# Block-sorted attention and a gated MLP on one core: a new order of issue for chunks 1 to 7, with packed score products

## The chip, the cores and the metric

The kernel runs on one core of a Trainium2 chip. A core has a matmul engine (TensorE, PE in the profile; its weight loads are listed apart as PEld), a vector engine (VectorE, DVE), an activation engine (ScalarE, ACT), a general-purpose engine (GpSimd, POOL) and an engine that here issues DMA transfers (SyncE, SP). Each of them runs its own list of instructions in the order in which the program gives them; semaphores hold an instruction until its inputs are there or its buffer is free. The metric is the time of one execution on the device in microseconds (us).

## The reference

The inputs are q, k and v of shape (4, 8, 768, 64), a net of 8x8 numbers for each of 32 heads, and two weight matrices. All is float32 outside the kernel; the kernel works in bfloat16 with float32 sums.

```python
P = sort_net                                   # 5 rounds of exp and row/column normalization
k_sorted = einsum('bhij,bhjcd->bhicd', P, k_b)  # blocks of 96 rows, mixed by P
v_sorted = einsum('bhij,bhjcd->bhicd', P, v_b)
scores = matmul(q_b, k_sorted^T) / sqrt(64)     # inside each block of 96 rows
attn = softmax(scores)
x = matmul(attn, v_sorted)                      # tokens x (8 heads * 64)
h = x @ w_in                                    # 512 -> 2048
out = (h * cos(h)) @ w_out                      # 2048 -> 512
```

## The kernel before

The 3072 tokens are worked on in eight chunks of 384 tokens; chunk n is one half of one batch, four blocks of 96 rows. Such a block of a chunk, with its eight heads, is called a unit (n, u). Batches 0 and 1 form group 0 (chunks 0 to 3), batches 2 and 3 form group 1 (chunks 4 to 7).

What is done for a unit, with the names of the kernel before and the lines that the profile gives:

- Scores, `qk`, `qk_half` or `s_ps`: eight matmuls (L405), one for each head. The turned queries lie in `q_turned` in such a way that for an even head rows 0 to 63 of the stationary operand hold the query and rows 64 to 127 are zero, and for an odd head the other way round; the moving operand (`keys_of`) has 128 rows of which the zeros leave 64 that count. Chunk 0 alone does its scores with operands of 64 rows (L681).
- The row maximum and the subtraction on DVE (L447 and L449, in chunks 0 and 1 L698 and L702), and the exponential on ACT (L467) into one of three `p_buf` tiles.
- The turn of the attention weights: by SP as a DMA transpose (L480), or on PE against the identity matrix (L713 or L493) with a copy out of PSUM by ACT.
- The product with the sorted values, `av_products` (L514), and on DVE the division by the row sums (L525, L527).
- The turn of x: by SP as a DMA transpose (L533), or on PE (L545, L722) with a copy.

For a chunk there follow eight steps `up` (L558; two column blocks of w_in each), a cosine on ACT (L562) and a product on DVE (L566) for each, and three output tiles `down` (L583) of sixteen matmuls each, with a copy out of PSUM and a store by SP (L573). The sorted keys and values are made by matmuls too (L375 and L425, L415), in pieces spread between the steps; `v_sort_g` makes those of group 1 with all 128 rows, two batches side by side.

PSUM has two pools: `big`, three tiles of two banks, and `acc`, two tiles of one bank.

The order is written out by hand, call after call for chunks 0 and 1, and with `moe_up`, `moe_down` and lists of calls for their slots for the others. PE works on the `up` and `down` steps of a chunk while the scores of the next one are made between them.

Two queues carry the transfers. POOL issues the loads: eight loads of 48 KB for the queries of a chunk from chunk 3 on (`load_q`, L129), and the keys and values of group 1 (`load_pair`, L92; two loads of 768 KB for keys, six of 256 KB for values). POOL also copies the loaded values into the order that the matmuls want (`v_permute`, L179), clears buffers, and has "holds": a copy of one column of a tile, which does nothing but keep POOL's later loads back until a transfer into that tile has landed (`hold`, L484; `hold_keys`, L393). SP issues the turns of q (`q_transpose_dma`, L149), of the attention weights and of x, and the stores.

The few lines that matter most for the order of POOL, in chunk 2:

```python
    p_hold(2, 2)
    for z in range(3, 6):
        load_pair(vbuf, vin_d, z * CD // 6, (z + 1) * CD // 6)
    load_q(4)
    v_permute(slice(0, 128))
```

Of the kernel before, what the change touches and what calls it, by code (L numbers as in the profile page):

```python
# [10 lines left out]
FP32 = mybir.dt.float32  # L11
# [3 lines left out]
AX = mybir.AxisListType  # L15


@with_exitstack
def kernel(
# [28 lines left out]
    IC = 4  # L48
# [323 lines left out]
    MH = H2 * IC  # L372

    def k_products(ps, t, c, rows, rhs, keys=kbuf):
        nc.tensor.matmul(  # L375
            ps[:, t], keys[rows, c * 2 * D:(c + 1) * 2 * D], rhs, start=True, stop=True)

    def k_sort_g(t0, eng, pool, tag):
        ps = pool.tile([128, 4, 4 * NB], FP32, name="ks", tag=tag)
        for t in range(4):  # L380
            k_products(ps, t, t0 + t, slice(0, 128), bds[1].rearrange("p x i -> p (x i)"),
                       pair)
        copy_on(
            eng, kT2[:, ::2, :, :, t0:t0 + 4].rearrange("p e b m t -> p b e m t"),
            ps.rearrange("p t (b e m) -> p b e m t", b=2, e=2))

    def k_swap(keys):
        nc.sync.dma_start(out=keys[:64, 1], in_=keys[64:, 0])
        nc.sync.dma_start(out=keys[64:, 1], in_=keys[:64, 2])

    def hold_keys():

        nc.gpsimd.tensor_copy(held[:], kT[1][:, 1, 0, :1])  # L393
# [14 lines left out]
    def v_cols(d, permuted):  # L408
        return vperm[:, d * blk:d * blk + 128] if permuted else vv[:, d]

    def v_sort_b(b, d0, nd, eng, pool, tag):
        ps = pool.tile([128, nd, 2 * NB], FP32, name="vs", tag=tag)
        rows, xs = slice(0, 64 + b * 64), slice(b * H, (b + 1) * H)
        for t in range(nd):
            nc.tensor.matmul(  # L415
                ps[:, t], v_cols(d0 + t, b == 1 or d0 + t >= D // 2)[rows],
                bdv[rows, xs].rearrange("p x i -> p (x i)"), start=True, stop=True)
        copy_on(
            eng, vS[0][:, b * 2 * NB:(b + 1) * 2 * NB, d0:d0 + nd],
            ps[:blk].rearrange("p t n -> p n t"))  # L420

    def v_sort_g(d0, nd, eng, pool, tag):
        ps = pool.tile([128, nd, 4 * NB], FP32, name="vs", tag=tag)
        for t in range(nd):
            nc.tensor.matmul(  # L425
                ps[:, t], v_cols(d0 + t, True), bds[1].rearrange("p x i -> p (x i)"),
                start=True, stop=True)
        copy_on(eng, vS[1][:, :, d0:d0 + nd], ps[:blk].rearrange("p t n -> p n t"))

    def v_at(g, b2, hp, h2, i):  # L430
        return (b2 * 2 + hp) * NB + h2 * nb + i


    LATE = 5
    s_t, pb, pT, xn_t = {}, {}, {}, {}
    xT = {}
    cnt = [0]

    def qk_part(n, u, part, pool, tag):
        w = len(part)  # L440
        sc = pool.tile([128, w, 512], FP32, name="sc", tag=tag)
        for h2 in range(H2):
            for e, hp in enumerate(part):
                scores(sc[:, e, h2 * 128:h2 * 128 + blk], n, u, h2, hp)
        scv = sc[:blk].rearrange("p e (h c) -> p (e h) c", c=128)[:, :, :blk]
        mx = small.tile([blk, w * H2], FP32, name="mx", tag="mx")
        nc.vector.reduce_max(mx[:], scv, axis=AX.X)  # L447
        s = s_t[n, u][:, part[0]:part[0] + w].rearrange("p e h c -> p (e h) c")
        nc.vector.tensor_tensor(s, scv, mx.to_broadcast(list(s.shape)), op=ALU.subtract)  # L449

    def qk(n, u):

        s_t[n, u] = sp.tile([blk, 2, H2, blk], FP32, name="s", tag="s")
        qk_part(n, u, [0, 1], big, "big")

    def qk_half(n, u, hp, pool=None, tag="acc"):

        if hp == 0:
            s_t[n, u] = sp.tile([blk, 2, H2, blk], FP32, name="s", tag="s")
        qk_part(n, u, [hp], pool or acc, tag)  # L460

    def expo(n, u, on_pe=False):
        p = p_bufs[cnt[0] % NP]
        cnt[0] += 1


        nc.scalar.activation(  # L467
            p[:, :, :blk], s_t.pop((n, u)).rearrange("p e h c -> p (e h) c"), AF.Exp,
            scale=scale)
        if n < LATE:  # L470
            t = ptp.tile([128, 2 * H2, blk], BF16, name="pT", tag="pT")
        else:

            z, w = (n * IC + u) % 8, 2 * H2 * blk
            t = vperm[:, z * w:(z + 1) * w].rearrange("p (a c) -> p a c", c=blk)
        pT[n, u] = t
        if on_pe:
            pb[n, u] = p
        else:
            nc.sync.dma_start_transpose(out=t[:], in_=p.rearrange("p a c -> p (a c)"))  # L480

    def hold(t):

        nc.gpsimd.tensor_copy(held[:blk], t[:blk, 0, :1])  # L484

    def p_hold(n, u):
        hold(pT[n, u])

    def p_transpose(n, u, eng, pool, tag):
        p = pb.pop((n, u))  # L490
        ps = pool.tile([128, 2 * H2, 128], BF16, name="pps", tag=tag)
        for a in range(2 * H2):
            nc.tensor.transpose(ps[:blk, a, :blk], p[:, a, :blk], ident[:blk, :blk])  # L493
        copy_on(eng, pT[n, u][:blk], ps[:blk, :, :blk])

    av_ps = {}

    def av(n, u, on_pe=False):
# [641 lines left out]
```

## Time and profile before

| | |
|---|---|
| median of 3 runs | 239.73 us (238.47, 239.73, 239.83) |
| span of the profiled execution, first to last instruction | 236.9 us |
| PE busy | 228.3 us, 96% |
| PEld, DVE, ACT, POOL busy | 61%, 72%, 65%, 39% |
| granted clock of the matmul engine, mean | 0.998 |
| bytes read from and written to HBM | 27.27 MB, 6.29 MB |

The execution that the profile shows is told by its span alone; a time of its own from start to end is not recorded beside it. The span is 2.8 us shorter than the median of the timed runs, and 1.6 us shorter than the fastest of them.

How to read the rows: an instruction group has its line, engine, operation, "written tile<-read tiles", shapes and count; after the bar stand its busy time in us, the mean duration of one in ns, and the idle time of the engine just before it with what ended that idle time. Matmuls are pipelined: each has a duration of some 200 to 380 ns from its start to its modelled end, but the next one starts long before that. So the time that a run of matmuls costs is read from start to start.

### The profile page before, as it was taken

Reading aid. Unit: us, or ns where it says so; the run is one execution under the profiler, and the core shown is the slowest. Engines: PE = TensorE matmul, PEld = TensorE weight load, DVE = VectorE, ACT = ScalarE, POOL = GpSimd, SP = SyncE. Lnnn points to the kernel's source line nnn. Section 1 sums busy time; section 2 is a strip of 40 time slices with the busy share of each in tenths; the row PEclk is TensorE's granted clock in tenths of the full one; section 3 lists DMA queues with packets and bytes.
Section 4 is the critical chain, followed back from the end, with each engine's and each line's share of the span. In section 5 each row is a group of like instructions: output and inputs, shape, how many; then the busy total and the mean of one; then the engine's idle time right before and its main releaser. Section 6 shows DMA issues by size and latency. Waiting matters only on the chain.

```text
span 236.9 us, 5429 instructions
## 1 busy us (share of the span) xinstructions
PE 228.3 (96%) x2230; PEld 144.0 (61%) x2230; DVE 171.1 (72%) x284; ACT 154.0 (65%) x205; POOL 93.4 (39%) x117
## 2 busy tenths in 40 slices
PE   8699999999999999999999999999999999999994
PEld 2368799567665656655666556655564565555553
DVE  5658976887789666893689976998698769535700
ACT  3356975588889747795688747673767376646611
POOL 7699994894970098940808000800000000000000
PEclk9999999999999999999999999999999999999999
DMA  7999999995899989869899938944972460341012
GB/s 97 203 199 205 203 224 211 148 201 167 102 117 183 146 155 136 160 150 184 95 104 101 116 64 150 209 68 91 119 216 46 80 192 3 55 133 47 0 44 89
DMA packets 66423, 30.89 MB, mean 130 GB/s; under 512 B 55136, under 2 KB 61920, under 8 KB 66144
## 3 DMA queue, kind: packets, MB, share of 16 engines
q0 software_dynamic: 24048, 13.64, 42.1%
q1 hardware_dynamic: 42064, 16.73, 33.4%
q8 instruction: 17, 0.28, 0.5%
q10 hardware_dynamic: 288, 0.20, 0.3%
q14 instruction: 6, 0.05, 0.1%
HBM read 27.27 MB, written 6.29 MB: 142 GB/s over the span
## 4 chain that ended last, share of the span: by engine, by line
PE 81%; DMA 6%; ACT 4%; DVE 4%; issue 3%; POOL 1%; SPq 0%; ACTq 0%; POOLq 0%
PE h L558 31%; PE o L583 21%; DMA pT<-p_buf 5%; PE h L735 5%; PE o L756 4%; PE sc L405 3%; PE av L514 3%; PE ks L375 2%; PE vs L662 2%; ACT p_buf L467 2%; PE o L1104 1%; PE vs L425 1%; PE pps L713 1%; DMA xT<-xn 1%; PE vs L238 1%
## 5 line engine op out<-in xcount | busy, mean ns | idle before, releaser
L558 PE MATMUL h<-xT,w_in_t 128*128 128x384 bf16 x448 | 78.4, 326 | 0.2 <-DMA xT<-xn 0.2
L583 PE MATMUL o<-w_out_t,gg 128*128 128x512 bf16 x320 | 76.5, 379 | 0.0
L566 DVE TENSOR_TENSOR gg<-c,h 128x768 bf16<-128x768 f32 x56 | 52.6, 949 | 18.8 <-ACT c L562 18.8
L562 ACT ACTIVATE c<-h,half_pi 128x768 f32<-128x768 f32 x56 | 50.4, 900 | 22.5 <-PE h L558 21.6
L558 PEld LDWEIGHTS <-w_in_t 128*128 128x128 bf16 x448 | 42.2, 98 | 26.5 <-issue 0.6
L583 PEld LDWEIGHTS <-gg 128*128 128x128 bf16 x320 | 29.1, 98 | 27.6
L467 ACT ACTIVATE p_buf<-s 96x768 bf16<-96x768 f32 x32 | 26.0, 840 | 4.4 <-DVE s L702 2.4
L179 POOL COPY vperm<-kv 64x1536 bf16<-64x1536 bf16 (+1 forms) x10 | 28.0, 2831 | 0.6 <-DMA kv<-in_v_dram 0.6
L449 DVE TENSOR_TENSOR s<-sc,mx 96x384 f32<-96x384 f32 (+1 forms) x33 | 24.3, 735 | 1.8
L447 DVE TENSOR_REDUCE mx<-sc 96x4 f32<-96x384 f32 (+1 forms) x33 | 24.0, 729 | 0.7 <-PE sc L405 0.7
L527 DVE TENSOR_TENSOR xn<-av,r 96x512 bf16<-96x512 f32 x32 | 22.0, 687 | 1.1
L525 DVE RECIPROCAL r<-av 96x8 f32<-96x8 f32 x32 | 6.4, 199 | 14.6 <-PE av L514 14.4
L129 POOL DMA_DIRECT2D kv<-in_q_dram x24 | 15.9, 674 | 0.7 <-issue 0.5
L405 PE MATMUL sc<-kTs,q_turned 128*128 128x96 bf16 x224 | 15.3, 206 | 0.1
L249 ACT COPY kv<-o 128x512 f32<-128x512 f32 (+2 forms) x10 | 5.3, 530 | 14.9 <-PE o L583 12.4
L405 PEld LDWEIGHTS <-q_turned 128*128 128x128 bf16 x224 | 12.6, 98 | 4.0 <-DVE s L449 0.4
L249 ACT CAST kTs<-ks 128x512 bf16<-128x512 f32 (+1 forms) x18 | 11.0, 632 | 5.7 <-PE ks L375 5.7
L756 PE MATMUL o<-w_out_t,gg 128*128 128x512 bf16 x48 | 11.4, 379 | 0.0
L251 DVE COPY kv<-o 128x512 f32<-128x512 f32 (+1 forms) x5 | 3.0, 602 | 11.4 <-PE o L1104 8.5
L129 POOL DMA_DIRECT2D q_mem<-in_q_dram x16 | 10.7, 684 | 1.2 <-DMA kv<-in_v_dram 1.0
L238 PE MATMUL idle<-warm 128*128 128x512 bf16 x29 | 8.5, 436 | 2.8 <-ACT q_turned L321 1.8
L735 PE MATMUL h<-xT,w_in_t 128*128 128x192 bf16 x128 | 11.1, 246 | 0.0
(119 smaller groups left out, 285.0 us busy)
## 6 DMA issues: line engine op xcount, KB each, us to landing
out_dram<-kv SPq DMA_DIRECT2D x12, 256.0 KB, 2.5
out_dram<-o_s SPq DMA_DIRECT2D x10, 256.0 KB, 2.7
w_in_t<-in_moe_w_in_dram POOLq DMA_DIRECT2D x4, 512.0 KB, 11.8
w_out_t<-in_moe_w_out_dram POOLq DMA_DIRECT2D x4, 512.0 KB, 12.6
kv<-in_k_dram POOLq DMA_DIRECT2D x2, 768.0 KB, 10.3
kv<-in_v_dram POOLq DMA_DIRECT2D x2, 768.0 KB, 13.1
pair<-in_k_dram POOLq DMA_DIRECT2D x2, 768.0 KB, 11.0
kv<-in_v_dram POOLq DMA_DIRECT2D x6, 256.0 KB, 5.4
```

Source lines behind the costliest of these rows:

```text
L129: nc.gpsimd.dma_start(out=q_heads[:, i, :, e], in_=src[:, ih * IC + i, :, e])
L179: nc.gpsimd.tensor_copy(dst, src)
L405: nc.tensor.matmul(out, q_of(n, hp)[:, x:x + 128], keys_of(n, u, h2, hp), start=True, stop=True)
L447: nc.vector.reduce_max(mx[:], scv, axis=AX.X)
L449: nc.vector.tensor_tensor(s, scv, mx.to_broadcast(list(s.shape)), op=ALU.subtract)
L467: nc.scalar.activation(p[:, :, :blk], s_t.pop((n, u)).rearrange("p e h c -> p (e h) c"), AF.Exp, scale=scale)
L527: nc.vector.tensor_tensor(xn.rearrange("p h e d -> p e h d"), avv[:, :, :, :D], r.to_broadcast([blk, 2, H2, D]), op=ALU.mult)
L558: nc.tensor.matmul(h[:, f2, :w], w_in_t[:, kk, f * 128:(f + 1) * 128], xT[n][:, kk], start=(kk == 0), stop=(kk == KC - 1))
L562: nc.scalar.activation(c[:], h[:, :, :w], AF.Sin, bias=half_pi[:, 0:1])
L566: nc.vector.tensor_tensor(gt[n, fp // 2][:, f:f + 2], c[:], h[:, :, :w], op=ALU.mult)
L583: nc.tensor.matmul(o[:], gt[n, f // 4][:, f % 4, ts * 128:(ts + 1) * 128], w_out_t[:, f, :], start=(f == 0), stop=(f == FC - 1))
L735: nc.tensor.matmul(o[:, part, f2 * w:(f2 + 1) * w], w_in_t[:, kk, f * 128:(f + 1) * 128], xT[0][:, kk, h * w:(h + 1) * w], start=(kk == 0) ...
```

## The change

The hand-written calls are replaced by one list of text lines, `PLAN`, and a loop that calls one function for each line. A line is an operation, its chunk and unit, and where it goes: `B` and `c` are the PSUM pools `big` and `acc`, `A` and `V` are ACT and DVE. `S` is a unit's scores, `M` the maximum, `X` the subtraction, `E` the exponential, `TP` and `TE` the turn on PE and its copy, `TD` the turn by DMA, `AV` the product with the values, `N` the division, `XP`, `XE` and `XD` the turn of x, `U`, `C`, `G` an `up` step with cosine and product, `D` four matmuls of a `down` tile, `O` and `W` its copy and its store; `QP`, `QE`, `QD` are the turns of q, `ks`, `kg`, `vb`, `vg` with `kse`, `kge`, `vbe`, `vge` the sorted keys and values and their copies, `Lq`, `Lpk`, `Lpv` the loads, `vp2` the copy of values into order, `hk`, `hp`, `hq` the holds; `nop` does nothing.

Chunk 0, and chunk 1 as far as its first `down` matmuls, are issued in the same order as before. From there on:

- Ten units have their scores from a new function `T`, which multiplies only the 64 rows that count: for the two heads of a pair one product uses rows 0 to 63 and the next rows 64 to 127, into two different PSUM banks. They stand on PE's list in five neighbouring pairs: (2,3) (2,2); (3,2) (3,3); (4,3) (5,0); (6,1) (6,0); (7,1) (7,2). The other units of chunks 1 to 7 keep products of 128 rows.
- One group of eight value columns of group 1 (`vg 0 8`) becomes `vgT`: two products of 64 rows in place of each one of 128 rows, one for each batch. It stands between the products of units (3,2) and (3,3).
- The turn of unit (1,0) is made by DMA (`TD 1 0`) in place of PE and a copy by ACT. On SP it stands behind the store `W 0 0`, which comes before `W 0 1` now.
- On every engine many operations change places by a few positions. No other operation is added or removed. Five copies change their engine: `kge 3`, `kge 6`, `vbe 0` go from ACT to DVE, `XE 2 1` and `O 3 2` from DVE to ACT; `kg 2`, `ks 0`, `vb 0` and `XP 3 1` change their PSUM pool.
- On SP the order of stores and turns changes too: W 0 0, TD 1 0, W 0 1 in chunk 1; QD 5 before W 2 2; W 3 2 before QD 6; W 4 0 before the turns of chunk 6; TD 6 1 before TD 6 0; XD 6 1 before XD 6 0.
- POOL's order from chunk 1 on was: zeros 3, Lq 3, hk, Lpv 0, Lpv 1, Lpv 2, zeros 4, hp 2 2, Lpv 3, Lpv 4, Lpv 5, Lq 4, vp2, ones 1, hp 3 3, Lq 5, hq 1, Lq 6, hq 0, Lq 7. It becomes: zeros 3, Lpv 2, Lq 3, zeros 4, Lpv 0, hk, Lpv 1, Lpv 3, Lpv 4, Lq 4, Lpv 5, vp2, hp 2 2, Lq 5, hp 3 3, ones 1, Lq 6, hq 1, Lq 7, hq 0.

```diff
--- before.py
+++ after.py
...
+PLAN = """\
...
+D 0 1 0
+D 0 1 1
+D 0 1 2
+X 1 2
+D 0 1 3
+M 1 0
+X 1 0
+M 1 3
+E 1 2 1
+E 1 0 2
+TP 1 2 B
+TE 1 2 A
+O 0 1 o A
+X 1 3
+E 1 3 0
+ks 4 B
+D 0 0 2
+D 0 0 3
+kse 4 V
+O 0 0 o V
+AV 1 2
+W 0 0
+S 1 1 B
+TP 1 3 c
+TD 1 0
+nop
+D 0 2 0
+D 0 2 1
+M 1 1
+X 1 1
+W 0 1
+TE 1 3 A
+D 0 2 2
+AV 1 3
+N 1 2
+N 1 3
+XP 1 2 B
+E 1 1 1
+TP 1 1 c
+XE 1 2 A
+AV 1 0
+D 0 2 3
+TE 1 1 A
+AV 1 1
+N 1 0
+XP 1 0 B
+N 1 1
+O 0 2 t A
+ks 3 B
+XE 1 0 A
+kse 3 A
+ks 2 c
+kse 2 A
+XP 1 3 c
+XE 1 3 V
+ks 1 B
+XP 1 1 B
+XE 1 1 V
+ks 0 c
+kse 1 A
+kse 0 A
+ks 5 B
+kse 5 V
+QP 2 0 c
+W 0 2
+QP 2 1 B
+QE 2 1 1 V
+zeros 3
+Lpv 2 6
+Lq 3
+zeros 4
+QE 2 1 0 V
+QE 2 0 1 V
+QE 2 0 0 V
+Lpv 0 6
+kswap 0
+hk
+U 1 0
+C 1 0
+G 1 0
+vb 0 B
+vbe 0 V
+vb 1 c
+vbe 1 A
+QD 3
+Lpv 1 6
+U 1 1
...
+S 2 1 c 1
+E 2 0 2
+nop
+TD 2 0
+M 2 1 1
+G 1 7
+X 2 1 1
+E 2 1 0
+TD 2 1
+D 1 0 0
+D 1 0 1
+T 2 3 B
+T 2 2 B
+M 2 2
+X 2 2
+nop
+D 1 0 2
+kg 0 c
+Lpv 3 6
+kge 0 A
+D 1 0 3
+O 1 0 o A
+M 2 3
+X 2 3
+Lpv 4 6
+E 2 2 1
+TD 2 2
+W 1 0
+kg 1 B
+D 1 1 0
+kg 4 B
+Lq 4
+Lpv 5 6
+kge 4 A
+kge 1 A
+vp2 0 128
+E 2 3 2
+hp 2 2
+D 1 1 1
+kg 2 c
+kge 2 A
+AV 2 0
+D 1 1 2
+D 1 1 3
+kg 3 B
+O 1 1 o A
+N 2 0
+W 1 1
+kge 3 V
+AV 2 1
+AV 2 2
+N 2 1
+TP 2 3 c
+N 2 2
...
+U 2 5
+C 2 5
+G 2 5
+kg 11 c
+kge 11 A
+kswap 1
+U 2 7
+C 2 7
+G 2 7
+nop
+U 2 6
+C 2 6
+E 3 0 0
+G 2 6
+S 3 1 c 1
+M 3 1 1
+X 3 1 1
+nop
+D 2 0 0
+E 3 1 1
+D 2 0 1
+D 2 0 2
+T 3 2 B
+vgT 0 8 B
+nop
+M 3 2
+T 3 3 B
+TD 3 0
+X 3 2
+TD 3 1
+D 2 0 3
+O 2 0 o A
+W 2 0
+M 3 3
+X 3 3
+E 3 2 2
+vge 0 8 A
+TD 3 2
+E 3 3 0
+D 2 1 0
+Lq 5
+D 2 1 1
+D 2 1 2
+vg 2 8 B
...
+TD 3 3
+D 2 1 3
+O 2 1 o A
+hp 3 3
...
+XE 3 3 V
+Lq 6
+nop
+D 2 2 3
+O 2 2 o V
+QD 5
+U 3 0
+C 3 0
+G 3 0
+hq 1
...
+D 3 0 0
+nop
+D 3 0 1
+X 4 2
+D 3 0 2
+nop
+E 4 0 1
+TD 4 0
+E 4 1 2
+nop
+TD 4 1
+T 4 3 B
+T 5 0 B
+E 4 2 0
+TD 4 2
+D 3 1 0
+M 4 3
+D 3 0 3
+X 4 3
+vg 15 4 B
+vge 15 4 A
...
+D 3 2 3
+O 3 2 v A
+W 3 2
+U 4 0
+QD 6
+Lq 7
...
+D 4 0 2
+nop
+T 6 1 B
+T 6 0 B
+M 6 0
+X 6 0
+D 4 0 3
...
+AV 6 2
+N 6 2
+XD 6 2
+nop
+T 7 1 B
+T 7 2 B
+D 5 1 2
...
+D 5 2 2
+XE 6 3 A
+U 6 0
+D 5 2 3
+O 5 2 v V
+E 7 1 2
+nop
+TD 7 1
+C 6 0
+G 6 0
+W 5 1
+U 6 2
...
+W 7 1"""
...
+    def T(n, u, pool, tag):
+        o = kept_tile(("s", n, u, None), pool, tag, [128, 2, 512], FP32, "sc")
+        for h2 in range(H2):
+            for hp in range(2):
+                rows, x = slice(hp * D, (hp + 1) * D), (u * H2 + h2) * blk
+                nc.tensor.matmul(
+                    o[:, hp, h2 * 128:h2 * 128 + blk], q_of(n, hp)[rows, x:x + 128],
+                    keys_of(n, u, h2, hp)[rows], start=True, stop=True)
...
+    def vgT(z, nd, pool, tag):
+        o = kept_tile(("vg", z), pool, tag, [128, 2, nd, 2 * NB], FP32, "vs")
+        for t in range(nd):
+            for b in range(2):
+                rows = slice(b * 64, (b + 1) * 64)
+                nc.tensor.matmul(
+                    o[:, b, t], v_cols(z * 4 + t, True)[rows],
+                    bds[1][rows, b * H:(b + 1) * H].rearrange("p x i -> p (x i)"),
+                    start=True, stop=True)
...
+    def E(n, u, z):
+        p = made["p", n, u] = p_bufs[z]
...
+    def TD(n, u):
+        nc.sync.dma_start_transpose(
+            out=p_to(n, u)[:], in_=made.pop(("p", n, u)).rearrange("p a c -> p (a c)"))
...
+    def Lpv(z, of):
+        load_pair(vbuf, vin_d, z * CD // of, (z + 1) * CD // of)
...
+    for line in PLAN.split("\n"):
+        name, *args = line.split()
+        given = []
+        for a in args:
+            given += words.get(a) or ((int(a),) if a.isdigit() else (a,))
+        calls[name](*given)
...
-    q_transpose(2, 1, (V, V), *B)
-    zeros_between(3)
-    load_q(3)
-    hold_keys()
-    load_pair(vbuf, vin_d, 0 * CD // 6, 1 * CD // 6)
-    load_pair(vbuf, vin_d, 1 * CD // 6, 2 * CD // 6)
-    load_pair(vbuf, vin_d, 2 * CD // 6, 3 * CD // 6)
...
-    expo(2, 3, True)
-    p_hold(2, 2)
-    for z in range(3, 6):
-        load_pair(vbuf, vin_d, z * CD // 6, (z + 1) * CD // 6)
-    load_q(4)
-    v_permute(slice(0, 128))
```

1372 lines of the change are left out of this document (817 added, 555 removed).

## Prediction

> **What bounds the kernel now.** I read the page first, then the chain of waits, then the timeline of PE around each place where it stops, and last the transfers. The first rows are the busy shares and the chain by engine, from the page.
>
> ```profile
> PE 228.3 (96%) x2230; PEld 144.0 (61%) x2230; DVE 171.1 (72%) x284; ACT 154.0 (65%) x205; POOL 93.4 (39%) x117
> ...
> PE 81%; DMA 6%; ACT 4%; DVE 4%; issue 3%; POOL 1%; SPq 0%; ACTq 0%; POOLq 0%
> ```
>
> PE is busy 96% of 236.9 us and carries 81% of the chain. A gain must take PE work away or close one of the few gaps; DVE and ACT have 28% and 35% of their time free. The next rows are PE's timeline at the four largest gaps of chunks 2 to 5 that the new order touches, and one more that it does not close.
>
> ```profile
> 72.82 1.89 PE L583 MATMUL o<-w_out_t,gg 128*128 128x512 bf16 x8
> 74.55 0.50 PE L405 MATMUL sc<-kTs,q_turned 128*128 128x96 bf16 x8
> 74.89 1.03 PE L583 MATMUL o<-w_out_t,gg 128*128 128x512 bf16 x4
> 75.94 0.38 PE L375 MATMUL ks<-bd,pair 128*128 128x128 bf16 x4
> ...
> 86.27 0.34 PE L545 MATMUL xps<-order,xn 96*128 96x96 bf16 x4
> 86.87 0.34 PE L545 MATMUL xps<-order,xn 96*128 96x96 bf16 x4 [0.27 <-DVE xn L527]
> ...
> 108.91 0.68 PE L514 MATMUL av<-vS,pT 96*128 96x65 bf16 x16
> 109.94 0.61 PE L425 MATMUL vs<-bd,vperm 128*128 128x128 bf16 x8 [0.34 <-ACT pair L249]
> 110.38 1.89 PE L583 MATMUL o<-w_out_t,gg 128*128 128x512 bf16 x8
> ...
> 140.03 0.43 PE L514 MATMUL av<-pair,pT 96*128 96x65 bf16 x8 [0.41 <-DMA pT<-p_buf]
> ...
> 165.78 0.59 PE L583 MATMUL o<-w_out_t,gg 128*128 128x512 bf16 x2
> 166.55 0.65 PE L558 MATMUL h<-xT,w_in_t 128*128 128x384 bf16 x3 [0.17 <-DMA xT<-xn]
> ```
>
> I count from start to start. Eight `down` matmuls take from 72.82 to 74.55, 0.216 us each; eight score products from 74.55 to 74.89, 42 ns each. Four `down` matmuls from 74.89 would be through at 75.75, but the next product starts at 75.94: 0.19 us are lost. In the same way four products of 42 ns from 86.27 lose 0.43, and two `down` matmuls from 165.78 lose 0.34. At 108.91 sixteen products with values stand; eight of that kind take 0.26 us (55.09 to 55.35, rows below), so 0.51 are lost before 109.94.
>
> **The packed products.** Here is PE's timeline in chunk 0, where products of 64 rows stand between products of 128 rows.
>
> ```profile
> 20.91 0.39 PE L238 MATMUL vs<-warm 128*128 128x512 bf16 x1
> 21.23 0.93 PE L662 MATMUL vs<-bdv,vperm 64*128 64x128 bf16 x14
> ...
> 22.06 0.40 PE L681 MATMUL sc<-kTs,q_turned 64*128 64x64 bf16 x14
> 22.39 0.28 PE L238 MATMUL pps<-warm 128*128 128x256 bf16 x1
> ```
>
> A unit's eight products of 128 rows take 0.34 us (above). The 64-row products step at (0.40 - 0.19)/13 = 16 ns: two of them run in the time of one. I take 42 ns for a pair of 96 columns, 0.17 us for a unit. A change between the two kinds has a price: from the 512-column product at 20.91 to the 64-row one it is 0.32 us, against the 0.216 of a stream, so 0.10; back, the last 64-row product starts at 22.27 and the next at 22.39, 0.09 more than a 64-column step. A neighbouring pair of units then costs 2 x 0.17 + 0.19 = 0.53 in place of 0.68: -0.15, five times -0.75 us. Bounds: -1.7 if the change were free, +0.95 if the halves did not overlap.
>
> `vgT`: eight products of 128 rows take from 109.94 to 110.38, 0.44 us; sixteen of 64 columns in pairs at 32 ns are 0.26: -0.18. It stands inside an island and pays no change of kind.
>
> **Gaps that close.** At 75.94 `kg 0` waited for the subtraction of (2,1); the list puts its maximum ahead of a product on DVE, so all 0.19 go. At 86.87 the division of (2,3) queued behind other DVE steps; that of (2,2) now comes early and one copy moves to ACT: 0.43 go. At 109.94 `vg 4` waited for a copy on ACT; the copies before it now start earlier: I keep 0.17, 0.34 go. At 166.55 a turn of x was late; half a unit's scores (0.17 us) now stands before that step: 0.2 go. Together -1.16 us, bounds 0 and -1.47. The gap at 140.03 stays.
>
> **The early turn by DMA.** Here is PE where the turned weights of (1,0) are used, with the turn of (1,1) before it and the next step behind, and SP.
>
> ```profile
> 54.73 0.52 PE L713 MATMUL pps<-ident,p_buf 96*96 96x96 bf16 x8
> 55.09 0.42 PE L514 MATMUL av<-vS,pT 96*128 96x65 bf16 x8
> 55.35 1.03 PE L756 MATMUL o<-w_out_t,gg 128*128 128x512 bf16 x4
> ```
>
> ```profile
> 49.20 2.44 SPq L573 DMA_DIRECT2D out_dram<-o_s  x2
> ```
>
> A turn on PE takes 0.36 us (54.73 to 55.09); that goes. Without the turn PE is at that product at 55.09 - 0.36 = 54.73. The DMA is queued behind `W 0 0`, which is the second of these two stores, issued at 51.31 (its copy on DVE ends then); so it goes out at about 51.7. What it meets there, from the answers for these stores, for the two key loads that POOL issued at 43.1 and 43.6, and for the later turns by DMA:
>
> ```profile
> L573 SPq DMA_DIRECT2D out_dram<-o_s x2: 332/350/368, 49.2 to 51.3; - x2
> ...
> DMA to landing us min/median/max: 5.9/6.6/7.4
> ```
>
> ```profile
> L92 POOL DMA_DIRECT2D pair<-in_k_dram x2: 553/558/562, 43.1 to 43.6; - x2
> ...
> DMA to landing us min/median/max: 9.2/11.0/12.7
> ```
>
> ```profile
> L480 SPq DMA_TRANSPOSE pT<-p_buf x11: 1212/1229/2490, 75.9 to 135.6; - x11
> ...
> DMA to landing us min/median/max: 2.8/3.0/4.5
> ```
>
> The key loads are in flight until 43.6 + 12.7 = 56.3, and the store issued at 51.31 landed at 57.2 (5.9 us). The turn takes the second store's place in the queue. If it met nothing it would land at 51.7 + 2.8 = 54.5, in time; by the store, its nearest row in place and time, at 56.8 or later. I take 56.8: PE waits 2.1 us, bounds 0 and 2.8. On PE all of chunk 1's rest is queued behind it. After that wait ACT has its copies (`O 0 2`, `XE 1 0`, `kse 3`, `kse 2`) in one go, and `ks 0` needs the bank that `kse 2` frees: I add 0.3 us, bounds 0 and 0.8.
>
> **POOL's loads without their hold.** These are POOL's timeline in chunk 2, SP's beside it, the answers for the turns of q of chunk 3, and the queues in 68 to 73 us.
>
> ```profile
> 60.74 5.33 POOL L129 DMA_DIRECT2D kv<-in_q_dram  x8
> ...
> 66.24 1.64 POOL L92 DMA_DIRECT2D kv<-in_v_dram  x3
> 67.85 1.88 POOL L137 MEMSET q_mem<- 96x1024 bf16 x2
> 82.91 0.18 POOL L484 CAST held<-pT 96x1 f32<-96x1 bf16 x1 [13.18 <-DMA pT<-p_buf]
> ```
>
> ```profile
> 75.93 5.14 SPq L480 DMA_TRANSPOSE pT<-p_buf  x3
> ```
>
> ```profile
> L149 SPq DMA_TRANSPOSE q_turned<-kv x2: 1577/2900/4222, 68.5 to 70.3; - x2
> ...
> DMA to landing us min/median/max: 6.2/6.4/6.7
> ```
>
> ```profile
> q0 software_dynamic: 424, 0.74, 98.0%
> q1 hardware_dynamic: 218, 0.06, 6.6%
> ```
>
> The hold (`hp 2 2`) kept POOL idle for 13.18 us, until the turns of chunk 2 had landed, and `Lpv 3` to `Lpv 5` and `Lq 4` came after. In the list that hold stands behind all of them and behind `vp2`; nothing else stops them. By the old durations `Lpv 2` starts at 60.74 (0.55 us), `Lq 3` ends at 66.6, `zeros 4` at 68.5, `Lpv 0`, the short `hk` and `Lpv 1` at 69.8, and `Lpv 3` goes out there. From 68 to 73 us three loads of values moved 0.74 MB, 0.15 MB/us, and the turns of q, issued at 68.5 and 70.3, got 0.06 MB: SP's transfers waited until POOL's were done. Four loads of values (1.0 MB) and `Lq 4` (0.38 MB), in flight from some 70 us, are through at about 79. The turn of (2,0), issued at 75.93, lands at 78.7 alone (2.8 us); its product stood at 79.53 and moves to some 79.2. The nearest row with such loads ahead is a store issued at 88.89:
>
> ```profile
> L573 SPq DMA_DIRECT2D out_dram<-o_s x1: 332/332/332, 88.9 to 88.9; - x1
> ...
> DMA to landing us min/median/max: 4.4/4.4/4.4
> ```
>
> ```profile
> out_dram<-c SPq DMA_DIRECT2D x1, 256.0 KB, 2.4
> ```
>
> That is 2.0 over a store of the same size with nothing ahead. With 2.0 more the turn lands at 80.7 and PE waits 1.5 us. Bounds: 0, and 4.5 if all that is queued goes first (to 79; then the turns of q, which needed from 73 to 70.3 + 6.2 = 76.5, so 3.5; then 1.2 of its own: 83.7).
>
> The Trainium skill has a rule against both waits: by "DMA: Bandwidth & Descriptors", Queues, rings and completion order, a DMA engine goes round robin between its queues, packet by packet. By it a turn would wait for one packet of a load and not for the load, and both waits would be near 0. The trace does not bear that out at 68 to 73 us, where the one queue had 98% and the other 6.6%.
>
> **The small rest.** `E 4 3` stands behind two copies of ACT, so the late turn at 140.03 gets later, and `U 6 0` is issued four `down` matmuls earlier, ahead of the landing of x: +0.4 together, bounds -0.4 and +1.5. `O 3 2` on ACT, the copies on DVE, the order of stores, and the earlier `Lq 5` to `Lq 7`: 0, covered by the 28% and 35% of free time and by loads that are wanted a chunk later.
>
> **The sum.** -0.75 - 0.18 - 1.16 - 0.36 + 2.1 + 0.3 + 1.5 + 0.4 = +1.85 us. The span is 236.9 and the median of the runs 239.73; I put the change on both: span 238.7, time 241.6 us.
>
> **The rivals.**
> - *Both turns land in time.* Then the two waits and the 0.3 behind the first fall away: 241.6 - 3.9 = 237.7 us, and 236.9 with the small rest at its lower end. For it: what the list removes on PE is certain. Against it: 5.9 to 7.4 us for stores at that very place.
> - *Only the first is late:* the turns of q get ahead of the loads, and the turn of (2,0) with them: 241.6 - 1.5 = 240.1.
> - *The whole backlog goes ahead of the turns of chunk 2.* The wait is 4.5 in place of 1.5: 244.6, slower. It decides as soon as `Lpv 3`, `Lpv 4` and `Lq 4` are queued before 75.9 and are served in the order of their issue. For it speak the 98% above, against it the 4.4 us of the store at 88.89.
> - *The halves do not overlap:* +0.95 in place of -0.75, 243.3. Against it speak the 16 ns of chunk 0.
>
> **Chances.** About 1% (2.4 us) is what this kernel's measurement can tell from no change. Forecast 0.34 (its own range 240.3 to 242.9, somewhat under half of it over 242.1, so 0.14); both in time 0.32 (half of it, 0.16, below 237.3, if a change of kind is cheaper too); first alone 0.18; backlog 0.12; no overlap 0.04. That makes 0.16 faster, 0.14 + 0.12 + 0.04 = 0.30 slower, and the other 0.54 within 1%. The range 236.8 to 244.0 leaves out the outer parts of the first and the third rival.
>
> **What would show it.** Ten units' products with a step near 21 ns and five islands at 0.53 us; the product of (1,0) waiting on `DMA pT<-p_buf` for about 2 us near 54.7; `Lpv 3` issued near 70 us and not behind a wait of 13 us; the turns of q of chunk 3 and of (2,0) landing late, and a wait of PE on `DMA pT<-p_buf` near 80 us. If the products of (1,0) and (2,0) start without a wait, the forecast is wrong and the first rival holds.

## The result and the profile after

The changed kernel took 253.31 us (median of 4 runs, 251.04 to 254.5) against 239.12 us of the kernel before: a ratio of 1.0581, 95% interval 1.0514 to 1.0649. It is 14.2 us slower, where +1.85 us (241.6 us) was forecast and the range ended at 244.0. A ratio and its interval, here and below, leave out executions more than 1.5% above the fastest of the same kernel; a median counts them all. The profiled execution took 251.04 us with a span of 249.2, so 12.3 us of span are to be explained.

The page after, with the same rows as of before, and the row of the granted clock in 40 slices:

```profile
PE 230.5 (92%) x2207; PEld 144.5 (58%) x2230; DVE 172.0 (69%) x285; ACT 153.2 (61%) x203; POOL 93.0 (37%) x117
...
PEclk9999999997999858999999999999999999999999
...
PE 66%; DMA 11%; issue 1%; POOL 1%; DVE 0%; ACT 0%; SPq 0%; ACTq 0%
```

PE's busy time rose by only 2.2 us, though PE has less to do; the chain now goes through DMA for 11% in place of 6%, and the clock is low in four slices. The waits of PE for transfers, and PE's timeline at the three long ones:

```profile
PE av L1445 <- DMA pT<-p_buf: 10.1, 3, 6.4
...
PE av L1445 <- DMA vperm<-p_buf: 0.7, 1, 0.7
```

```profile
54.38 0.52 PE L1427 MATMUL pps<-ident,p_buf 96*96 96x96 bf16 x8
56.90 0.43 PE L1445 MATMUL av<-vS,pT 96*128 96x65 bf16 x8 [2.00 <-DMA pT<-p_buf]
...
89.14 0.65 PE L1445 MATMUL av<-vS,pT 96*128 96x65 bf16 x8 [6.35 <-DMA pT<-p_buf]
89.60 3.60 PE L1550 MATMUL o<-w_out_t,gg 128*128 128x512 bf16 x8
...
147.48 0.42 PE L1445 MATMUL av<-pair,pT 96*128 96x65 bf16 x8
149.63 0.43 PE L1445 MATMUL av<-pair,pT 96*128 96x65 bf16 x8 [1.74 <-DMA pT<-p_buf]
```

The three are the products of (1,0), (2,0) and (4,2). Behind the second one, eight `down` matmuls are busy for 3.60 us; before, eight took 1.89. The stretches behind the first two waits, with the length and PE's busy time first and the granted clock (PEclk) behind the engines:

```profile
57.00:60.00 3.00, 2.94 (x36) 2.11 (x37) 1.60 (x4) 1.01 (x2) 0.00 (x0) 0.58 0.00 0
89.20:93.20 4.00, 4.00 (x18) 1.79 (x19) 0.89 (x2) 1.28 (x2) 1.05 (x1) 0.50 1.00 179
93.20:96.00 2.80, 2.75 (x32) 2.32 (x32) 2.20 (x5) 1.35 (x2) 2.80 (x2) 0.67 0.25 94
```

The clock lost 3.00 x 0.42 + 4.00 x 0.50 + 2.80 x 0.33 = 4.2 us. With 10.1 us of waits that is 14.3 us, against 12.3 in the span (behind the first row the clock stays low up to 60.9 us, which adds some 0.4). So what the new list saves on PE seems to be there, some 2 us net; this is what is left over of a sum, not a measurement of its own.

Why the turn of (2,0) came late is seen in SP's timeline, and in the queues from 81 to 84 us (packets, MB, share of 16 engines' time):

```profile
71.21 7.90 SPq L994 DMA_TRANSPOSE q_turned<-kv  x2
...
79.20 6.62 SPq L1418 DMA_TRANSPOSE pT<-p_buf  x3
```

```profile
q1 hardware_dynamic: 1219, 0.31, 81.6%
q0 software_dynamic: 1244, 0.16, 80.1%
```

POOL had issued its four loads of values and q for chunk 4 from 71.07 us on. SP needed until 79.1 to issue the two turns of q of chunk 3, one of them 5.9 us long, so the turn of (2,0) went out at 79.20 and landed at 89.09. From 81 to 84 us SP's queue (q1) and POOL's (q0) moved almost the same count of packets. It isn't so everywhere: from 77 to 80 us, with loads of values on their way, POOL's queue moved 265 packets (0.48 MB) and SP's 131 (0.03 MB), and from 51.8 to 53.0 us, behind the issue of the turn of (1,0), POOL's moved 37 packets of its key load (0.23 MB) and SP's none.

### The profile page after: what moved, and what is told of

The parts are those of the page before. It is cut to its first block, busy times and chain, and to the rows that moved or that the text cites. A ratio compares the mean times of both kernels' runs of the same rounds, so it can differ in the third digit from the quotient of the medians.

```text
span 249.2 us, 5406 instructions
## 1 busy us (share of the span) xinstructions
PE 230.5 (92%) x2207; PEld 144.5 (58%) x2230; DVE 172.0 (69%) x285; ACT 153.2 (61%) x203; POOL 93.0 (37%) x117
## 4 chain that ended last, share of the span: by engine, by line
PE 66%; DMA 11%; issue 1%; POOL 1%; DVE 0%; ACT 0%; SPq 0%; ACTq 0%
PE h L1505 28%; PE o L1550 25%; DMA pT<-p_buf 8%; PE av L1445 3%; PE sc L1344 2%; DMA vperm<-p_buf 2%; PE ks L1225 2%; PE o L1641 1%; PE xps L1479 1%; PE vs L1316 1%; DMA kTs<-kTs 1%; PE sc L1371 1%; POOL vperm L1024 1%; PE vs L1293 0%; DVE kTs L1096 0%
## 5 line engine op out<-in xcount | busy, mean ns | idle before, releaser
L1550 PE MATMUL o<-w_out_t,gg 128*128 128x512 bf16 x348 | 86.8, 387 | 1.1 <-issue 0.2
L1550 PEld LDWEIGHTS <-gg 128*128 128x128 bf16 x368 | 33.7, 100 | 33.8 <-issue 1.9
L1385 DVE TENSOR_REDUCE mx<-sc 96x8 f32<-96x768 f32 (+1 forms) x41 | 31.6, 771 | 1.9 <-PE sc L1344 1.1
L1445 PEld LDWEIGHTS <-pT 96*128 96x128 bf16 (+1 forms) x160 | 8.0, 109 | 13.0 <-DMA pT<-p_buf 11.3
L1445 PE MATMUL av<-vS,pT 96*128 96x65 bf16 (+1 forms) x128 | 7.3, 209 | 8.4 <-DMA pT<-p_buf 8.3
L1094 ACT COPY kv<-o 128x512 f32<-128x512 f32 (+2 forms) x11 | 5.9, 537 | 14.8 <-PE o L1550 12.2
L1094 ACT CAST kTs<-ks 128x512 bf16<-128x512 f32 (+1 forms) x16 | 9.8, 635 | 3.3 <-PE ks L1225 3.2
L1083 PE MATMUL idle<-warm 128*128 128x512 bf16 x28 | 9.7, 492 | 2.2 <-ACT q_turned L1166 1.2
L1094 ACT COPY xT<-xps 128x384 bf16<-128x384 bf16 (+1 forms) x11 | 5.5, 508 | 9.9 <-PE xps L1479 9.8
L1094 ACT CAST pair<-vs 96x512 bf16<-96x512 f32 (+1 forms) x12 | 8.7, 726 | 3.9 <-PE vs L1316 3.9
## 6 DMA issues: line engine op xcount, KB each, us to landing
kv<-in_k_dram POOLq DMA_DIRECT2D x2, 768.0 KB, 10.1
```

Source lines behind the costliest of these rows:

```text
L1094: eng.copy(dst, src)
L1385: nc.vector.reduce_max(mx[:], s_view(n, u, hp), axis=AX.XY if n < 2 else AX.X)
L1445: nc.tensor.matmul(a[:w, hp, h2 * (D + 1):(h2 + 1) * (D + 1)], pt[:blk, e * blk:e * blk + w], vS[g][:, v_at(g, b2, hp, h2, ih * IC + u), : ...
L1550: nc.tensor.matmul(out_ps[n, ts][:], gt[n, q][:, f % 4, ts * 128:(ts + 1) * 128], w_out_t[:, f, :], start=(f == 0), stop=(f == FC - 1))
```

## The experiments

All times are compared with runs of the kernel before on the same chip (238.6 to 239.5 us as a median). Two runs that are compared with each other can come from different chips; then their ratios say more than the difference of their times.

### The two late turns, one at a time

```diff
 S 1 1 B
+TP 1 0 B
 TP 1 3 c
-TD 1 0
+TE 1 0 A
```

> The changed kernel with one thing undone: the turn of (1,0) is on PE again, with its copy on ACT. In the changed kernel's trace PE waits 2.2 us for that turn, and its clock is 0.58 of full from 57 to 60 us behind the wait (1.26 us lost); the turn on PE takes 0.36 us. Theory A (both late turns and the low clock behind each make the loss): 253.3 - 2.2 - 1.3 + 0.4 = 250.2 us, a granted clock near 1 from 57 to 60 us, and the long wait near 82 us stays at about 6.5 us. Rival B (the landing near 89 us is tied to loads whose start does not move with PE, so the second wait grows by what the first gives up): 253 us, second wait 9 us or more. Rival C (the clock is cut by something else than the wait): 251.5, clock still low near 57 us.

254.15 us in the median, but the four executions lie far apart (249.23, 254.06, 254.25 and 257.27), so no ratio is given and the size of the gain is open. The trace is of the one of 249.23, whose span of 247.5 us is 1.7 shorter than the changed kernel's. In it the wait and the low clock of chunk 1 are gone, as theory A has it: the clock is 1.00 from 57 to 60 us. The second wait is 5.78 us, so rival B, where it grows, falls.

```profile
57.00:60.00 3.00, 3.00 (x82) 2.59 (x79) 2.50 (x5) 2.98 (x7) 1.46 (x2) 1.00 0.27 94
```

```profile
85.43 0.65 PE L1446 MATMUL av<-vS,pT 96*128 96x65 bf16 x8 [5.78 <-DMA pT<-p_buf]
```

But later waits came up that the changed kernel didn't have, a turn of x and a turn of chunk 6:

```profile
PE av L1446 <- DMA pT<-p_buf: 7.5, 2, 5.8
PE h L1506 <- DMA xT<-xn: 1.7, 1, 1.7
PE av L1446 <- DMA vperm<-p_buf: 1.6, 1, 1.6
```

The edit itself puts eight products and eight weight loads more on PE ahead of these places. What a count of instructions ahead can do to later waits is followed up below.

```diff
 TD 2 2
+hp 2 2
+Lpv 3 6
+Lpv 4 6
```

(`Lpv 3`, `Lpv 4` and the hold were taken from their places; `Lq 4` and `Lpv 5` follow behind.)

> The changed kernel with POOL's hold for the turn of (2,2) ahead of the loads of values 3 to 5 and of q for chunk 4 again; the rest, the early turn by DMA too, as changed. Theory A: the wait of 6.5 us at the product of (2,0) falls to under 0.5, and with it the low clock behind it (0.50 from 89.2 to 93.2 and 0.67 to 96 us: 2.0 + 0.9 us lost): 253.3 - 6.3 - 2.9 = 244 us. Rival B (the turns of q and the three loads of values ahead of them are enough to make the turn late): a wait of 2 us or more stays and the time is 247 or more. Rival C (a large part of the loss is in the packed products and their changes of kind): 246 or more with no such wait.

244.31 us (241.97 to 246.67), 1.0195 (1.0126 to 1.0264). That is theory A's number: PE's timeline has no wait for the turn of (2,0) any more and the clock stays up there, 9.0 us in all (9.2 by the ratios). So POOL's order is the main cause. The early turn still costs a wait of 2.23 us in this trace, and a wait of 1.79 us for a turn of chunk 4 has half clock behind it.

```profile
85.00 0.39 PE L1225 MATMUL ks<-bd,pair 128*128 128x128 bf16 x4
85.40 0.95 PE L1445 MATMUL av<-vS,pT 96*128 96x65 bf16 x16
```

> The changed kernel with both undone: the turn of (1,0) on PE and the hold ahead of the loads. Theory A: the sum of the two, 253.3 - 3.1 - 9.2 = 241.0 us, since a wait of 1.9 us for a turn of chunk 4 and one of 0.8 us for a turn of chunk 5 or 6 remain. The forecast's other terms alone (packed products, group of values, closed gaps, without either wait and with the turn on PE) would give 239.1 - 0.75 - 0.18 - 1.16 + 0.4 = 237.4. Rival C (packed products cost time): 243 or more.

(Both edits.) 243.72 us (242.66 to 245.51), 1.0211 (1.0157 to 1.0264): 2.7 above theory A, by the ratios not below the run with the hold alone, and as high as rival C has it (packed products that cost time; the next run bears on that). The same late waits as in the first run:

```profile
PE av L1446 <- DMA pT<-p_buf: 2.7, 3, 1.7
PE h L1506 <- DMA xT<-xn: 1.7, 1, 1.7
PE av L1446 <- DMA vperm<-p_buf: 1.4, 1, 1.4
```

These are 5.8 us of waits for turns in the fastest of the four executions, with the turn of (1,0) on PE and no loads in the way. They are followed up below.

```diff
-T 2 3 B
-T 2 2 B
+S 2 3 B
+S 2 2 B
```

(and so for all ten units)

> As the run with both undone, and the ten units' scores with products of 128 rows again, at the same places of the list. Theory A (a neighbouring pair of packed units saves 0.15 us): 0.75 us above the run with both undone, and PE's steps show 0.34 us a unit in place of about 0.17 with 0.10 and 0.09 at the ends. Rival C (the change of kind costs more than the halves save): equal to it or faster, by up to 1 us.

244.42 us (244.16 to 247.6), 1.0263 (1.0197 to 1.0329): 0.7 above the run with both undone, as theory A has it. Rival C, by which it would be below, finds no support here, but the two intervals overlap, so this alone doesn't settle what the pairs give.

### Which loads, and how queues share

Here the run with both undone is the base, and one kind of load goes ahead of the hold again.

```diff
 TD 2 2
-hp 2 2
 Lpv 3 6
 Lpv 4 6
+Lpv 5 6
+hp 2 2
 Lq 4
```

> As the run with both undone (turn of (1,0) on PE, hold ahead of the loads), but the loads of values 3 to 5 (0.77 MB in packets of 2,048 bytes) go out ahead of the hold; q for chunk 4 stays behind it. Theory A1 (a queue takes its turn packet by packet, so small packets of a turn each wait for one large packet of a load): during the some 4 us in which those loads move, the turns of q and of (2,0) get almost nothing, and the product of (2,0) waits 2 to 4 us, with a lower clock behind it: 246 to 249 us. Theory A2 (what is issued first is served first, by bytes): as much, for 0.77 MB at 0.15 to 0.2 MB/us. Rival D (the loads of values cost nothing, q for chunk 4 is the cause alone): no wait, 243.7.

251.95 us in the median, but its four executions lie far apart (247.15 to 254.27), so no ratio is given. In the profiled one, 252.63, the product of (2,0) waits 8.58 us and the two turns of q land 16.2 and 17.5 us after their issue. Even the fastest is 3.4 us above the base, so rival D (the values cost nothing) falls; the size is not settled. The queues from 76 to 79 us moved similar counts of packets and six times as many bytes for the loads as for the turns:

```profile
q0 software_dynamic: 174, 0.32, 82.3%
q1 hardware_dynamic: 213, 0.05, 26.1%
```

```diff
 TD 2 2
+Lq 4
 hp 2 2
 Lpv 3 6
 Lpv 4 6
-Lq 4
```

> As the run with both undone, but q for chunk 4 (0.38 MB in packets of 128 bytes) goes out ahead of the hold; the loads of values 3 to 5 stay behind it. Theory A1 (packet by packet): while both queues have work, each gets the same count of packets, some 410 per us, in place of the 1,000 per us that a turn of q moves alone; the turns of q of chunk 3 (3,064 packets) and that of (2,0) take some 4 us longer, and the product of (2,0) waits 2 to 4 us: 246 to 249 us. Theory A2 (served in the order of issue): no packet of a turn moves until the load is through, half the bytes of the other run and so half its wait: 1 to 2 us. Rival D' (q for chunk 4 costs nothing): 243.7.

248.94 us (248.36 to 251.0), 1.043 (1.0374 to 1.0486): 5.2 over the base. That is theory A1's time; its wait was too small, 5.92 us in place of 2 to 4 (in the profiled execution, the longest of the four). The queues from 78 to 81 us decide between A1 and A2:

```profile
q1 hardware_dynamic: 1262, 0.32, 80.1%
q0 software_dynamic: 1263, 0.16, 79.2%
```

1,262 packets against 1,263: in this stretch the queues share by the count of packets, whatever was issued first, and A2 falls. Packets are 256 bytes in the turns and 128 in q's loads, so here the turn has twice the bytes. Beside loads of values, whose packets have 2,048 bytes, a similar count leaves a turn far less (the rows of the run before this one). And in other stretches SP's queue got nothing at all: in the kernel before, from 68.5 to 72 us, POOL's queue moved 288 packets and SP's none, though a turn of q was issued at 68.5. Why is open.

### The clock behind a wait

```diff
 def AV(n, u):
     ...
+    if (n, u) == (2, 0):
+        keep_warm(28, a[:, 0])
```

> The changed kernel as it is, with 28 idle products of 512 columns (6.05 us at full clock) put on PE ahead of the product of (2,0), into the bank that this product then writes over. PE has work in the wait for the turn; the turn itself lands where it did. Theory A (the low clock follows from PE standing idle): the granted clock behind the wait is 1.0 in place of 0.50 (4 us) and 0.67 (2.8 us), and the time falls by some 2.9 us: 250.4. Rival C (the clock is cut by something else, as load on the chip): clock still 0.5 behind the product of (2,0), 253.3 or, where the idle products outlast the wait, more. The 56 added instructions also move the places where PE's instructions are fetched, which can shift later waits by up to 2 us either way; so the clock and PE's steps from 89 to 96 us decide, not the time alone.

Nothing of the result is left out; the 28 products are added. 247.21 us (245.97 to 249.59), 1.0354 (1.0281 to 1.0427). The turn landed at 88.43 us, about as late as before, but the clock behind it is 1.00:

```profile
57.00:60.00 3.00, 2.92 (x31) 1.96 (x32) 1.29 (x4) 0.70 (x2) 0.00 (x0) 0.59 0.00 1
85.00:89.00 4.00, 4.00 (x21) 1.76 (x19) 0.00 (x0) 0.49 (x1) 0.00 (x0) 1.00 1.68 143
93.00:96.00 3.00, 3.00 (x31) 1.69 (x28) 1.47 (x4) 1.27 (x2) 3.00 (x2) 1.00 0.11 40
```

The first row is the control: behind the wait of chunk 1, which was not filled, the clock is 0.59 as in the changed kernel. So the low clock follows from PE standing idle, and rival C falls. The spans of the two profiled executions differ by 249.2 - 246.3 = 2.9 us, theory A's number, but that is in part a coincidence: the same product, at 96.93 us in the changed kernel, starts at 94.83 here, 2.1 us earlier, and the rest comes from shorter later waits. The medians differ by 6.1, and what the other 3 are is not settled. So the row of the clock decides here, not the time.

### The fetches of PE's instructions

In the run with both undone the products behind the three late waits stand near 137, 167 and 186 us. The transfers of that run from 135 to 138 us have one packet in a queue of their own, and the same is so at 166.1 and 185.3:

```profile
q1 hardware_dynamic: 1280, 0.31, 92.5%
q8 instruction: 1, 0.02, 1.9%
```

It is 16 KB of instructions. The turn in whose way it falls lands after 4.2 to 4.4 us.

```diff
-    keep_warm(15, big.tile([128, 512], FP32, name="idle", tag="big"))
+    keep_warm(60, big.tile([128, 512], FP32, name="idle", tag="big"), 128)
```

> As the run with both undone, with one difference at the start: the warming products are 60 of 128 columns in place of 15 of 512, the same columns in all, which puts 90 PE instructions more ahead of everything. In the run with both undone three waits of 1.8, 1.9 and 1.6 us (for turns used at 136.9, 167.1 and 185.6 us) each stand where a transfer of 16 KB of PE's instructions (at 136.5, 166.1, 185.3) falls into a turn, which then lands after 4.2 to 4.4 us in place of 2.4 to 2.9. Theory F (these fetches make the waits, and so the time depends on the count of instructions ahead): the fetches move some 4 to 6 us earlier, and at least two of the three waits fall below 0.7 us: 240 to 241.5. Rival G (the list leaves the turns too little time in any case): the three waits stay within 0.5 us, 243.7.

240.33 us (median of 10), 1.0052 (1.0017 to 1.0087): 3.4 us below the run with both undone, by 90 PE instructions more at the start (the same columns, in smaller products). The fetches stand at 129.4, 143.7, 161.6 and 177.0 us now. In the stretch from 135 to 138 us there is no such packet any more. PE's waits for transfers (behind the colon us in total, times, the longest):

```profile
PE sc L1345 <- DMA kTs<-kTs: 1.1, 1, 1.1
PE av L1446 <- DMA vperm<-p_buf: 0.9, 1, 0.9
PE av L1446 <- DMA pT<-p_buf: 0.7, 2, 0.6
```

The wait of 1.65 us at 138.75 is down to 0.16, that for x is gone, that of chunk 6 too; new ones of 0.9 and 1.1 stand where fetches (161.6 and 60.9) now meet a turn of chunk 5 and the swap of the sorted keys of chunk 2. Theory F holds and G falls: the waits go where the fetches go.

### The packed pairs alone

The kernel before, with one part of the change: ten units in five neighbouring pairs, with 64 rows.

```diff
-S 2 2 B
+T 2 2 B
+T 2 3 B
 ...
-S 2 3 B
```

> The kernel before with one part of the change alone: the same ten units, brought next to each other in five pairs, with products of 64 rows; every other step where it was, and as many PE instructions as before, so that the fetches of PE's instructions stay at their places. Theory A (a packed pair takes 0.53 us in place of 0.68, and PE's saving reaches the end): 238.8 - 0.75 = 238.1 us. Theory H (PE is through earlier, but then waits longer for turns that land when they did, above all for those with a fetch in them): PE's products are 0.75 us shorter and the waits longer by 0.4 to 0.75, 238.5 to 239. Rival C (a change of kind costs more than the halves save): 239.5 or more.

239.95 us (12 executions), 1.0036 (1.0007 to 1.0066): not a gain but a small loss. PE's timeline shows where it can come from: the pair itself is as short as forecast (128.00 + 8 x 0.216 = 129.73 to 130.30, 0.57 us for two units), and PE then stands at the turns of (4,1) and (4,2).

```profile
128.00 1.89 PE L1517 MATMUL o<-w_out_t,gg 128*128 128x512 bf16 x8
129.82 0.55 PE L1338 MATMUL sc<-kTs,q_turned 64*128 64x96 bf16 x16
130.30 1.90 PE L1517 MATMUL o<-w_out_t,gg 128*128 128x512 bf16 x8
...
134.24 1.89 PE L1517 MATMUL o<-w_out_t,gg 128*128 128x512 bf16 x8
137.51 0.43 PE L1412 MATMUL av<-pair,pT 96*128 96x65 bf16 x8 [1.38 <-DMA pT<-p_buf]
138.42 0.43 PE L1412 MATMUL av<-pair,pT 96*128 96x65 bf16 x8 [0.48 <-DMA pT<-p_buf]
138.69 3.08 PE L1517 MATMUL o<-w_out_t,gg 128*128 128x512 bf16 x8
```

A fetch stands at 134.9, and the turns of (4,1) and (4,2) land 5.2 and 4.8 us after their issue. Behind the waits eight `down` matmuls take 3.08 us in place of 1.89: behind these two short waits the clock is low as well (0.50 from 139.2 to 142.6 us, which loses 1.7 us). The trace is of one of four executions of 241.2 to 241.9 us, whose mean granted clock is 0.991 to 0.993. The other eight took 239.06 to 240.21 us (median 239.6) with a mean clock of 0.998 or more; how long PE waits in them no trace shows.

Two gaps were closed on top of that, without a load or a turn moved:

```diff
 S 2 1 c 1
-G 1 7
 M 2 1 1
+G 1 7
 ...
-XE 2 1 V
+XE 2 1 A
```

> As the run with the pairs alone, and two local steps of the change for gaps that the prediction named: the maximum of (2,1) ahead of a product on DVE (the gap of 0.19 us ahead of kg 0), and the copy XE 2 1 on ACT in place of DVE (the gap of 0.43 us behind the division of (2,3)). No loads and no turns are moved. Theory A: 0.4 us below the run with the pairs alone, 237.7. Theory H (what PE gains waits at the next turn): within 0.2 us of it.

240.2 us, 1.0045 (1.0014 to 1.0075), within 0.3 us of the pairs alone: theory H. In this trace the product of (2,0) waits 1.4 us, with a fetch at 78.3.

### The same kernels with the fetches moved

> The kernel before with the warming products as 60 of 128 columns in place of 15 of 512, 90 PE instructions more ahead of everything, nothing else. Theory F1 (the fetches of PE's instructions cost wherever a turn is used with little slack): the wait of 0.58 us at 139.4, behind a turn with a fetch in it, goes, and others come where a fetch now falls into a turn; the time moves by 0.3 to 1 us, either way. Theory F2 (the list of before leaves its turns more time than the changed list does, so it is hardly touched): within 0.5 us of 238.8, and no wait for a turn over 0.7 us.

(The edit of the warming products, on the kernel before.) 238.48 us (median of 10), 0.9969 (0.9948 to 0.999). The time moved by 0.6 us, and the wait of 0.41 us at 140.03, behind a turn with a fetch in it, is gone. Both theories allow that; the runs with 30 instructions, below, decide.

> The pairs alone, with 90 PE instructions more at the start (60 warming products of 128 columns). Compare with the kernel before with the same 90, 0.9969 of before. If the fetch made the loss (theory F), the wait of 1.5 us for the turn of (4,1) goes and the pairs give most of their 0.75 us: 0.9969 x 239.1 - 0.6 = 237.8 us. If the turns are late in any case (theory H), a wait of 0.5 us or more stays in chunk 4 and the time is 238.5 or more.

(The same edit on the pairs alone.) 237.64 us, 0.9925 (0.9901 to 0.9949). Against the kernel before with the same 90 instructions the pairs give 238.48 - 237.64 = 0.84 us (by the ratios 0.9969 - 0.9925, 1.05 us; the two runs are from different chips and their intervals just touch): about what the prediction had. PE's timeline at the place that waited:

```profile
134.71 0.42 PE L1412 MATMUL av<-pair,pT 96*128 96x65 bf16 x8
135.19 1.67 PE L1517 MATMUL o<-w_out_t,gg 128*128 128x512 bf16 x7
136.70 0.94 PE L1412 MATMUL av<-pair,pT 96*128 96x65 bf16 x16
137.47 1.89 PE L1517 MATMUL o<-w_out_t,gg 128*128 128x512 bf16 x8
```

No fetch falls into these turns (they stand at 129.7 and 143.8), which land after 2.8 to 3.1 us, and PE doesn't wait.

> The pairs and the two closed gaps (maximum of (2,1) ahead of a product, copy XE 2 1 on ACT), with the same 90 PE instructions more. Theory F: 0.2 to 0.4 us below the pairs alone with 90 more, 237.5. Theory H: what PE gains in chunk 2 waits at the turns of chunk 2 (the run without the 90 waited 1.56 us there, with a fetch in the turn): within 0.2 us of it or above.

237.2 us (236.9 to 237.63), 0.9909 (0.9875 to 0.9943): 0.9% below the kernel before, and 0.4 us below the pairs alone with the same shift. The two intervals overlap, so that the two gaps give their share here is likely rather than shown; in the trace, the gap of 0.26 us ahead of the turn of x at 87.59 us of the pairs alone is gone.

> The pairs alone, with 30 PE instructions more at the start (30 warming products of 256 columns). The fetches stand some 1 to 2 us earlier than in the run of the pairs alone (134.9 there): still near the turns of chunk 4. Theory F: the time depends on which turn a fetch falls into; a wait of about 1 us or more in chunk 4 where a fetch falls into the turn of (4,0), (4,1) or (4,2), else none; 238 to 240.5. Theory H: as the pairs alone, 239.5 to 240.5 in any case.

> The kernel before with the same 30 PE instructions more, nothing else. Theory F: within 0.7 us of 239.1, as its fetches fall. The difference to the pairs with 30 more is what the pairs give at this place of the fetches: -0.75 if nothing waits, 0 or above where a new wait takes it.

(30 warming products of 256 columns, on the pairs alone and on the kernel before.) 241.96 us, 1.0102 (1.0064 to 1.0141), and 241.51 us (of the ten executions that the ratio takes), 1.0091 (1.0061 to 1.0121). The kernel before loses 0.9% by 30 instructions at its start; the forecast for it (within 0.7 us) was too narrow, and theory F2, that it is hardly touched, falls. A fetch falls into a turn of x of chunk 5 in both (166.5 and 164.5 us), and in the pairs alone one (136.2) into the turns of chunk 4 as well. The pairs give nothing at this place of the fetches. What a fetch does is seen in the queues of the pairs alone from 136.0 to 137.2 us:

```profile
q1 hardware_dynamic: 117, 0.03, 190.6%
q8 instruction: 1, 0.02, 4.6%
```

While the one large packet moves, the 117 packets of the turns take 1.2 x 16 x 1.906 / 117 = 0.31 us each; with no fetch, 1,262 took 80.1% of 3 us, 0.03 us each (rows above).

## Why the prediction was wrong

- **Packed products, -0.75.** The price was right: in the changed kernel a pair takes 0.54 us, forecast 0.53. From the `down` matmul at 167.71, two of 0.216 and then the pair, to 168.68:

```profile
167.71 0.59 PE L1550 MATMUL o<-w_out_t,gg 128*128 128x512 bf16 x2
168.23 0.51 PE L1371 MATMUL sc<-kTs,q_turned 64*128 64x96 bf16 x16
168.68 1.90 PE L1550 MATMUL o<-w_out_t,gg 128*128 128x512 bf16 x8
```

  The step that failed is the one from PE's time to the end: a shorter PE brings the next product nearer to its turn. With the fetches at three places the pairs gained 0.84 us, where no fetch met a tight turn, and lost 0.83 (239.95 against 239.12) and 0.45 (241.96 against 241.51), where one did. The rival that the halves do not overlap falls.
- **The early turn, +2.1 and +0.3.** It came out right: landing forecast at 56.8, measured at 56.85 (51.81 + 5.05), wait 2.0 to 2.2 us. The mechanism, a queue in front of the turn, was right too: no packet of SP's queue moved before 53.8 us. The tenth is partly luck, since the prediction works 56.8 out from no row (a turn that meets nothing gave 54.5, the store beside it 57.2). What was missing is the clock behind the wait, 1.3 us up to 60 us; the +0.3 can't be told apart from it.
- **POOL's loads, +1.5, bounds 0 and 4.5.** This is the failed step that carries the result. The mechanism, the loads in the way of the turns, was right, and the rival of the whole backlog came nearest. The size was wrong three times over. The turn was taken to be issued at 75.93 and to land at 80.7; SP was held by the turns of q until 79.1, and the turn landed at 89.09. The wait was sized by a store of 2,048-byte packets, while a turn comes in packets of 256 bytes, and where both queues had small packets they moved equal counts of them. And the clock was not counted. 6.35 us of wait, outside the bound of 4.5, and 2.9 of clock stood in place of 1.5; putting the hold back gave back 9.0 us.
- **The rule of taking turns.** The prediction set the rule of the Trainium skill ("DMA: Bandwidth & Descriptors", Queues, rings and completion order) aside because one queue had 98% and the other 6.6% at 68 to 73 us. The counts bear that reading out: from 68.5 to 72 us POOL's queue moved 288 packets and SP's none, and SP's 218 all came after 72. At 78 to 81 us of the run with q early the packets stand 1,262 to 1,263, so the rule holds there. Where it holds, its use in the prediction was wrong: a turn does not wait for one packet, but for one packet for each of its own. In other stretches beside large packets the counts are unequal (265 to 131, 37 to 0), and why is open.
- **The clock.** No step had it. The longest wait of PE quoted for before is 0.41 us; the forecast put long waits in and left the speed behind them at full. By the clock rows 2.9 us hang on the second wait alone; in the filled run 2.1 of them show in PE's timeline. The Trainium skill ("TensorE: Matmul & The Clock Gate", Part 1) has a clock of half speed behind an idle window of some 3.4 us; that half is what 3.60 us for eight `down` matmuls show, but here a wait of 2.0 us, and two of 1.38 and 0.48, brought it too, while in the run with both undone three waits of 1.4 to 1.7 us did not (mean clock 1.000).
- **The small rest, +0.4.** The late turns of chunk 4 cost a wait of 1.74 us. A fetch began at 147.3 us in that turn, which landed 4.48 us after its issue, and the runs with the fetches moved put such waits down to this; no step had it.
- **Gaps closed, -1.16.** The two in chunk 2 are not in the trace after, but there they stand behind the long wait, so it is no test of them; in the run with the pairs, the two gaps and the shift they are closed. The one at `vg 4` is 0.13 us after and 0.46 or more in the runs with the turn on PE, save the one with the fetches moved; and the kernel before, in its own order with 30 or 90 instructions more, doesn't have it either. The one ahead of `U 5 0` became 1.7 us in the runs with the turn on PE. So these last two hang on where the fetches and the turns fall as much as on the order.

## What to carry to other kernels

Where PE is 96% busy and every product waits for a transfer that lands just in time, PE's time and the end are not the same thing: for each saving, write down the slack of the next turn, and take 1.4 us off it (4.3 less 2.9, the medians below) for a fetch of instructions that may fall into it. A load put ahead of small-packet transfers can cost more than its bytes say (the 0.38 MB of q in 128-byte packets cost 5.2 us). And a wait of PE of 2 us or more cost itself and a stretch of about half clock behind it here; shorter ones did so only sometimes. And a list tuned to a few tenths should be timed with its fetches at two or three other places (some idle instructions at its start) before an edit of under 1% is called good or bad.

## What the runs showed that was not expected

- **The count of instructions ahead moves the time.** The kernel before took 239.12 us, with 90 PE instructions more at its start 238.48, and with 30 more 241.51; the changed list with both edits undone took 243.72 and, with 90 more, 240.33. Over all profiled runs, turns of weights issued after 100 us landed 2.9 us (median of 257) after their issue, and 4.3 us (median of 83) where a fetch began 0.2 to 3.5 us after it.
- **Two queues that both have small packets share by their count, here to 0.1%:** 1,262 packets of 256 bytes against 1,263 of 128. Beside packets of 2,048 bytes and more SP's queue got a similar count in one stretch and none in others.
- **Waits far shorter than expected can halve the clock:** 1.38 and 0.48 us, one product apart, were followed by 3.4 us at 0.50; the row starts 0.6 us ahead of that stretch and has 0.59:

```profile
138.60:142.00 3.40, 3.40 (x22) 1.58 (x19) 1.18 (x3) 0.00 (x0) 0.00 (x0) 0.59 0.20 38
```

The stretches at half clock in the traces are some 3.4, 6.8 or 10.2 us long (139.2 to 142.6 us here, 84.8 to 95.0 in the changed kernel), so each of the short waits that brought one cost some 1.7 us on top of itself (half of 3.4). What decides whether a wait of 1.5 us does so was not tried.
